# Sixteen attention units of a decode step: fourteen of them as one hardware loop of seven rounds, with the value and MLP products at other places

## The chip, the cores and the metric

The kernel runs on one core of one Trainium2 chip. Time is device time in microseconds (us) of one execution. In the profile, PE is TensorE (PEld its weight loads), DVE is VectorE, ACT is ScalarE, POOL is GpSimd and SP is SyncE, which here only issues transfers. PEclk is the clock granted to TensorE, 1.00 being full speed.

## What is computed

Two branches meet in the output. A is attention for one new token per batch (2 batches, 32 query heads, 8 KV heads, 32,768 cached positions, head size 128); B is a small MLP whose result gates A. All inputs are bf16.

```python
xn = layernorm(x)                                   # x: 2 x 1 x 512
q = xn @ wq                                         # 512 x 4096, 32 heads of 128
scores = einsum("bhqd,bhkd->bhqk", q, k) * 128**-0.5
p = softmax(scores);  o = einsum("bhqk,bhkd->bhqd", p, v)
s = o @ wo                                          # 4096 x 512
# branch B for a sequence of one token: its shifted parts are zero, so x1 = xn
h2 = gelu(layernorm(xn) @ w3) @ w4                  # F = 1792
out = x + s * silu(xn + h2)
```

K and V are 134 MB each; together with the weights the core reads 280.5 MB from HBM.

## The kernel before

**Units and buffers.** A unit is one batch and one KV head: 16 units, numbered 0 to 15, batch changing fastest. Each needs its K (8.39 MB) and its V (8.39 MB). `kbuf` has three chunks of half a K each. An even unit's K lies in chunks 0 and 1, an odd unit's in 1 and 2; even units work on chunk 1 first and then chunk 0, odd units on chunk 1 and then 2. So the next K can be loaded as soon as the first half of this K has been read. There is one V buffer, which first holds wq, w3 and w4. The last unit's V goes in three pieces into `kbuf` chunks 0 and 1, and wo in four pieces into chunk 2.

**The stream.** SP issues all large transfers in one order: half of K(0), wq, the other half, w3, w4, then K(1), V(0), K(2), V(1), ... K(15), V(14), V(15), wo. An instruction in that queue waits until its buffer has been read: a K for DVE's transposes (L320), a V for PE's value products (L348).

**A unit.** `k_job` takes a half of K in four pieces; DVE transposes a piece (L320) into one of two `ktb` buffers, and PE forms the scores from it in eight matmuls (`scores`, L268), one piece behind DVE. I call these eight matmuls a score block; a unit has eight blocks. After the last, DVE takes the maximum (L282), PE and DVE spread it over the partitions (mT L287, gm, gx, bc L298, nb L302), ACT does the exponential (L305) and DVE transposes the result (pT, L309). `v_job` then multiplies pT with V (64 matmuls of 16 rows in four column strips, L348), one unit behind: PE does the scores of unit n+1 and then the value products of unit n. `unit_end` copies the sum (acs, L365) and normalizes it (L369 to L376).

**The order** of all instructions is written out by hand in Python: the list `order` with `needs` for the transfers, and lists `waiting` and `glue` for score blocks and softmax steps that are put behind other work. Everything is unrolled: PE's program has 2,499 matmuls.

**The ends.** `q_job` (L404 to L418) makes the queries once wq is there; `mlp_job` (L437 to L469) runs both MLP products after unit 0's scores; V(0) may be loaded only after it. At the end `v_job` of unit 15, `o_final` (L382 to L388) and `wo_job` (128 matmuls, L395) follow, and two DVE instructions (L503, L505) and the output transfer.

Of the kernel before, what the change touches and what calls it, by code (L numbers as in the profile page):

```python
# [8 lines left out]
F32 = mybir.dt.float32  # L9
# [7 lines left out]
GT = 16  # L17
# [6 lines left out]
def kernel(  # L24
# [36 lines left out]
    units = [(b, g) for g in range(Hkv) for b in range(B)]  # L61
    NU = len(units)
# [8 lines left out]
    pt_pool = ctx.enter_context(tc.tile_pool(name="probT", bufs=2))  # L71
    tmp = ctx.enter_context(tc.tile_pool(name="tmp", bufs=3))
    sm_pool = ctx.enter_context(tc.tile_pool(name="small", bufs=3))
    sc_psp = ctx.enter_context(tc.tile_pool(name="sc_ps", bufs=2, space=bass.MemoryType.PSUM))
# [17 lines left out]
    def place(n, c):  # L92
        return (n % 2 + c) * CW

    def halves(n):
        return (0, 1) if n % 2 else (1, 0)

    loads = [("K", 0, 1), ("wq",), ("K", 0, 0), ("w3",), ("w4",)]
    for n in range(NU):
        if n + 1 < NU:  # L100
            loads += [("KK", n + 1), ("V", n)]
        else:
            loads += [("Z", n, c) for c in range(NCH)]
    wo_cuts = [0, NR // 2, NR - 6, NR - 2, NR]
    loads += [("wo",)]
    tiles = {}
    done = set()
    needs = {("V", 0): ("w4",), ("Z", NU - 1, 0): ("K", NU - 2, 0),
             ("Z", NU - 1, 1): ("K", NU - 1, 0), ("wo",): ("K", NU - 1, 1)}
    for n in range(1, NU):  # L110
        needs["V", n] = ("V", n - 1)
        needs["KK", n] = ("K", n - 1, halves(n - 1)[0])

    def issue_ready():
        while loads and needs.get(loads[0], None) in (done | {None}):
            issue(loads.pop(0))

    def issue(what):
        kind = what[0]
        if kind in ("wq", "V"):  # L120
            t = vslot.tile([128, NCH * CW], BF16, tag="v", name=f"slot_{kind}")
        elif kind in ("w3", "w4"):
            t = tiles[("wq",)]
        elif kind == "K":
            t = kbuf[:, place(0, what[2]):place(0, what[2]) + CW]
        elif kind == "KK":
            t = kbuf[:, place(what[1], 0):place(what[1], 0) + NCH * CW]
        else:
            c = 2 if kind == "wo" else what[2]
            t = kbuf[:, c * CW:(c + 1) * CW]  # L130
        if kind in ("K", "KK", "V", "Z"):
            b, g = units[what[1]]
            src = A_k_cache if kind[0] == "K" else A_v_cache
            sv = src[b, g, :, :].rearrange("(p t) d -> p (t d)", p=128)
            if kind in ("KK", "V"):
                nc.sync.dma_start(out=t[:, :], in_=sv)
            else:
                c0, w = what[2] * CW, CW
                if what == ("Z", NU - 1, NCH - 1):
                    w = w // 2  # L140
                for w0 in range(0, CW, w):
                    nc.sync.dma_start(out=t[:, w0:w0 + w], in_=sv[:, c0 + w0:c0 + w0 + w])
        elif kind == "wq":
            nc.sync.dma_start(
                out=t[:, 0:DK * HD].rearrange("p (k f) -> p k f", k=DK), in_=wq_v)
        elif kind == "wo":
            for r0, r1 in zip(wo_cuts, wo_cuts[1:]):
                nc.sync.dma_start(out=t[:, r0 * D:r1 * D], in_=wo_v[:, r0 * D:r1 * D])
        elif kind == "w3":
            nc.sync.dma_start(  # L150
                out=t[:, W3:W3 + DK * Fdim].rearrange("p (k f) -> p k f", k=DK), in_=w3_v)
        else:
            nc.sync.dma_start(
                out=t[:, W4:W4 + FK * D].rearrange("p (f d) -> p f d", f=FK), in_=w4_v)
        tiles[what] = t

    order = []
    for w in loads:
        order += [("K", w[1], c) for c in halves(w[1])] if w[0] == "KK" else [w]
    issue(loads.pop(0))  # L160
# [6 lines left out]
    issue_ready()  # L167
# [10 lines left out]
    qp = pers.tile([128, 4, B, Hkv, rep], BF16)  # L178
# [41 lines left out]
    layernorm(xn, xf, "ln1")  # L220
    xn_bf = tmp.tile([B, D], BF16, tag="row", name="xn_bf")
# [21 lines left out]
    g_sb = pers.tile([B, D], F32)  # L243
    g4 = pers.tile([128, 128], F32)
    nc.gpsimd.memset(g4[:, :], 0.0)


    unit_st = {}
    waiting = []
    glue = []  # L250

    def state(n):
        if n not in unit_st:
            unit_st[n] = {
                "sc": sc_psp.tile([128, NHALF, GT * 32], F32, tag="sc", name="sc"),
                "pT": None,
            }
        return unit_st[n]

    def scores(n, grp, ktb):  # L260
        b, g = units[n]
        st = state(n)
        half, sl = grp // NS, grp % NS
        sc = st["sc"]
        kv = ktb.bitcast(BF16).rearrange("p (t wb k two) -> p wb two t k", wb=2, k=32, two=2)
        off = 32 - rep - rep * sl
        for k in range(4):
            nc.tensor.matmul(  # L268
                sc[:, half, :].rearrange("p (t k) -> p t k", k=32),
                lhsT=qz[:, n % 2, k, off:off + 128],  # L270
                rhs=kv[:, k // 2, k % 2, :, :],
                start=(sl == 0 and k == 0), stop=(sl == NS - 1 and k == 3),
            )
        if sl == NS - 1 and half == halves(n)[1]:
            softmax_front(n)

    def softmax_front(n):
        st = state(n)
        if n + 2 < NU:
            place_q(n + 2)  # L280
        m1 = sm_pool.tile([128, 1], F32, tag="m1", name="m1")
        nc.vector.tensor_reduce(  # L282
            out=m1[:, :], in_=st["sc"][:, :, :].rearrange("p x k -> p (x k)"), axis=AX.X, op=ALU.max)
# [12 lines left out]
        def step2():  # L296
# [6 lines left out]
            S1 = sm_pool.tile([128, 1], F32, tag="S1", name="S1")  # L303
            pr = p_pool.tile([128, NHALF * GT * 32], BF16, tag="p", name="pr")
            nc.scalar.activation(  # L305
                out=pr[:, :], in_=st["sc"][:, :, :].rearrange("p x k -> p (x k)"), func=ACT.Exp,
                bias=nb[:, 0:1], scale=inv_sqrt_dh, accum_out=S1[:, :])
            pT = pt_pool.tile([128, NHALF * GT, 32], BF16, tag="pT", name="pT")
            nc.vector.transpose(out=pT[:, :, :].rearrange("p t r -> p (t r)"), in_=pr[:, :])  # L309
            st["pT"] = pT  # L310
            Sm = sm_pool.tile([128, rep], F32, tag="Sm", name="Sm")
            nc.vector.tensor_scalar_mul(out=Sm[:, :], in0=headm[:, :], scalar1=S1[:, 0:1])
            st["Sm"] = Sm
# [4 lines left out]
    def transposed(n, grp, kw):  # L318
        ktb = kt_pool.tile([128, KG * GT * DW], U32, tag="ktb", name="ktb")
        nc.vector.transpose(out=ktb[:, :], in_=kw)  # L320
        for x in range(KG):
            waiting.append((n, grp + x, ktb[:, x * GT * DW:(x + 1) * GT * DW]))
# [5 lines left out]
    def k_job(n, c):  # L328
        kw = kbuf[:, place(n, c):place(n, c) + CW].bitcast(U32)
        for blk in range(0, NB, KG):  # L330
            transposed(n, c * NB + blk, kw[:, blk * GT * DW:(blk + KG) * GT * DW])
            if n == 0 and c == 1 and blk < KTB * KG:
                if blk == (KTB - 1) * KG:
                    q_job()
                continue
            flush(LAG * KG)
            if glue:
                glue.pop(0)()

    def v_job(n, t, c0, c1):  # L340
        nx = NB // 4
        vv = t[:, :].rearrange("p (x i t d) -> p x t i d", i=4, t=GT, d=Dh)
        for x in range(c0 * nx, c1 * nx):
            half, r0 = x * 4 // NS, x * 4 % NS * rep
            pT = unit_st[n]["pT"]
            for u in range(GT):
# [3 lines left out]
                    lhsT=pT[:, half * GT + u, r0:r0 + 16],  # L350
# [4 lines left out]
        if c1 == NCH:  # L355
            unit_end(n)
# [4 lines left out]
    def unit_end(n):  # L361
        b, g = units[n]
        st = unit_st.pop(n)
# [3 lines left out]
        def step1():  # L367
            ot = mi_psp.tile([128, 2 * rep], F32, tag="mi", name="ot")
            nc.tensor.matmul(ot[:, rep:2 * rep], lhsT=ones_f[:, :], rhs=st["Sm"][:, :], start=True, stop=True)  # L369
            for i in range(4):  # L370
# [6 lines left out]
                out=oQ[:, b, g * rep:(g + 1) * rep], in0=ot[:, 0:rep], in1=rc[:, :], op=ALU.mult)  # L377
# [12 lines left out]
    def wo_job():  # L390
        w = tiles[("wo",)]
# [7 lines left out]
    def q_job():  # L399
        qT_ps = mi_psp.tile([128, Hq * B], F32, tag="mi", name="qT")  # L400
        for h in range(Hq):
            for k in range(DK):
                w = tiles[("wq",)]
                nc.tensor.matmul(  # L404
                    qT_ps[:, h * B:(h + 1) * B],
                    lhsT=w[:, k * HD + h * Dh:k * HD + (h + 1) * Dh],
# [5 lines left out]
        for k in range(4):  # L412
# [5 lines left out]
        nc.vector.tensor_copy(  # L418
            out=qp[:, :, :, :, :].rearrange("p k b g h -> p k (b g) h"),
            in_=qp_ps[:, :, :].rearrange("p (k u) h -> p k u h", k=4))  # L420
        place_q(0)
        place_q(1)

    def place_q(n):
        b, g = units[n]
        for i in range(4):
            c0 = 32 - rep + 32 * i
            nc.scalar.copy(  # L428
                out=qz[32 * i:32 * i + 32, n % 2, :, c0:c0 + rep], in_=qp[32 * i:32 * i + 32, :, b, g, :])

    def mlp_job():
        w3 = tiles[("w3",)][:, W3:W3 + DK * Fdim].rearrange("p (k q f) -> p k f q", k=DK, f=FK)
        w4 = tiles[("w4",)][:, W4:W4 + FK * D].rearrange("p (f d) -> p f d", f=FK)
        hT_ps = mi_psp.tile([128, FK * B], F32, tag="mi", name="hT")
        for f in range(FK):
            for k in range(DK):
# [5 lines left out]
                )  # L442
        hf = pers.tile([128, FK * B], F32)
        nc.vector.tensor_copy(out=hf[:, :], in_=hT_ps[:, :])
# [10 lines left out]
        h2_ps = mi_psp.tile([B, D], F32, tag="mi", name="h2")  # L455
        for f in range(FK):
            nc.tensor.matmul(  # L457
                h2_ps[0:B, :],
                lhsT=h_bf[:, f * B:(f + 1) * B],
                rhs=w4[:, f, :],  # L460
                start=(f == 0), stop=(f == FK - 1),
            )
        t_f = tmp.tile([B, D], F32, tag="row", name="t_f")
# [74 lines left out]
```

## Time and profile before

| | |
|---|---|
| median of 3 runs | 659.57 us (659.34 to 659.73) |
| the profiled execution's own time | 659.42 us |
| its span, first to last instruction | 657.6 us |
| PE busy | 375.9 us (57%) |
| DVE busy | 362.2 us (55%) |
| ACT busy, POOL busy | 38.5 us (6%), 2.4 us |
| read from HBM | 280.50 MB, 427 GB/s over the span |
| chain that ended last | DMA 67%, DVE 13%, PE 12% |

A column like "22.25 (x141)" in the windows view is busy time and number of instructions of an engine in that stretch; its last three columns are PEclk, the mean busy share of the 16 DMA engines (packets that overlap count twice, so it can pass 1) and GB/s. In the timeline a line has start, duration, engine, source line, operation, output<-input, count, and in brackets the idle time before it and what ended it. In the list of waits the three numbers are us in total, times and the longest.

### The profile page before, as it was taken

Reading aid. Unit: us, or ns where it says so; the run is one execution under the profiler, and the core shown is the slowest. Engines: PE = TensorE matmul, PEld = TensorE weight load, DVE = VectorE, ACT = ScalarE, POOL = GpSimd, SP = SyncE. Lnnn points to the kernel's source line nnn. Section 1 sums busy time; section 2 is a strip of 40 time slices with the busy share of each in tenths; the row PEclk is TensorE's granted clock in tenths of the full one; section 3 lists DMA queues with packets and bytes.
Section 4 is the critical chain, followed back from the end, with each engine's and each line's share of the span. In section 5 each row is a group of like instructions: output and inputs, shape, how many; then the busy total and the mean of one; then the engine's idle time right before and its main releaser. Section 6 shows DMA issues by size and latency. Waiting matters only on the chain.

```text
span 657.6 us, 5890 instructions
## 1 busy us (share of the span) xinstructions
PE 375.9 (57%) x2595; PEld 166.6 (25%) x2595; DVE 362.2 (55%) x312; ACT 38.5 (6%) x104; POOL 2.4 (0%) x10
## 2 busy tenths in 40 slices
PE   0583846638184673908558282754818376480865
PEld 0341322313132231303223031321303122130333
DVE  6183928547382754729356382936638284562821
ACT  1012010100001010000101000010100101000000
POOL 1000000000000000000000000000000000000000
PEclk9997987969587795968869596896959679695985
DMA  9999999999999999999999999999999999999995
GB/s 383 422 440 448 439 439 431 416 446 428 442 439 415 447 419 439 439 424 442 424 442 439 415 446 424 446 443 403 443 438 444 442 396 438 446 443 446 392 428 245
DMA packets 6125, 280.88 MB, mean 427 GB/s; under 512 B 714, under 2 KB 724, under 8 KB 980
## 3 DMA queue, kind: packets, MB, share of 16 engines
q1 hardware_dynamic: 6056, 280.50, 98.7%
q8 instruction: 20, 0.33, 0.2%
q14 instruction: 5, 0.04, 0.0%
q10 hardware_dynamic: 44, 0.01, 0.0%
HBM read 280.50 MB, written 0.00 MB: 427 GB/s over the span
## 4 chain that ended last, share of the span: by engine, by line
DMA 67%; DVE 13%; PE 12%; issue 6%; ACT 1%; ACTq 0%; SPq 0%; DVEq 0%
DMA kbuf<-in_A_k_cache_dram 60%; DVE ktb L320 12%; PE sc L268 10%; DMA kbuf<-in_A_wo_dram 4%; DMA slot_wq<-in_A_wq_dram 3%; PE h L457 1%; PE qT L404 1%; PE hT L437 1%; PE s_ps L395 0%; ACT L305 0%; DVE pT L309 0%; ACT pr L305 0%; ACTq L469 0%; ACT qz L428 0%; DVE g_sb L467 0%
## 5 line engine op out<-in xcount | busy, mean ns | idle before, releaser
L268 PE MATMUL sc<-ktb,qz 128*128 128x512 bf16 x1024 | 269.4, 412 | 228.1 <-DVE ktb L320 226.5
L320 DVE STREAM_TRANSPOSE ktb<-kbuf 128x2048 uint32<-128x2048 uint32 x128 | 285.0, 2282 | 156.1 <-DMA kbuf<-in_A_k_cache_dram 129.0
L268 PEld LDWEIGHTS <-qz 128*128 128x128 bf16 x1024 | 103.7, 102 | 387.4 <-issue 295.8
L348 PE MATMUL acc<-slot_V,pT 128*16 128x512 bf16 x960 | 54.4, 379 | 0.0
L428 ACT COPY qz<-qp 32x16 bf16<-32x16 bf16 x64 | 12.9, 201 | 444.4 <-PE sc L268 424.7
L282 DVE TENSOR_REDUCE m<-sc 128x1 f32<-128x1024 f32 x16 | 19.6, 1225 | 31.8 <-PE sc L268 31.8
L365 DVE COPY acs<-acc 128x512 f32<-128x512 f32 x16 | 11.1, 692 | 46.4 <-PE acc L348 46.4
L348 PEld LDWEIGHTS <-pT 128*16 128x16 bf16 x1024 | 24.5, 91 | 41.0 <-issue 14.5
L309 DVE STREAM_TRANSPOSE pT<-pr 128x1024 bf16<-128x1024 bf16 x16 | 19.9, 1245 | 22.6 <-ACT pr L305 22.6
L305 ACT ACTIVATE pr<-sc,nb 128x1024 bf16<-128x1024 f32 x16 | 17.8, 1113 | 134.3 <-DVE nb L302 134.3
L371 PE MATMUL ot<-sel,acs 128*128 128x4 f32 x128 | 17.4, 259 | 0.3 <-DVE acs L365 0.3
L371 PEld LDWEIGHTS ot<-sel,acs 128*128 128x128 f32 x128 | 16.4, 200 | 0.4 <-DVE acs L365 0.4
L298 PE MATMUL bc<-ones_f,gx 1*128 1x1 f32 x32 | 6.0, 256 | 17.9 <-DVE gx L292 17.9
L404 PE MATMUL qT<-xT,slot_wq 128*128 128x2 bf16 x128 | 3.6, 165 | 12.2 <-DMA slot_wq<-in_A_wq_dram 12.2
L348 PE MATMUL acc<-kbuf,pT 128*16 128x512 bf16 x64 | 6.4, 557 | 6.6 <-DMA kbuf<-in_A_v_cache_dram 5.0
L298 PEld LDWEIGHTS bc<-ones_f,gx 1*128 1x128 f32 x32 | 4.7, 182 | 20.9 <-DVE gx L292 20.9
L302 DVE TENSOR_SCALAR nb<-bc 128x1 f32<-128x1 f32 x16 | 2.5, 158 | 7.5 <-PE bc L298 7.5
L404 PEld LDWEIGHTS <-slot_wq 128*128 128x128 bf16 x128 | 3.5, 104 | 12.2 <-DMA slot_wq<-in_A_wq_dram 12.2
L369 PE MATMUL ot<-Sm,ones_f 128*128 128x4 f32 x32 | 6.4, 269 | 0.0
L457 PE MATMUL h<-slot_wq,h_bf 128*2 128x512 bf16 x14 | 4.8, 513 | 1.6 <-DVE h_bf L454 1.6
L369 PEld LDWEIGHTS ot<-Sm,ones_f 128*128 128x128 f32 x32 | 5.0, 195 | 1.1 <-issue 0.8
L410 DVE CAST q_sb<-qT 128x64 bf16<-128x64 f32 x1 | 0.2, 225 | 8.8 <-PE qT L404 8.8
(71 smaller groups left out, 65.2 us busy)
## 6 DMA issues: line engine op xcount, KB each, us to landing
kbuf<-in_A_k_cache_dram SPq DMA_DIRECT2D x2, 4096.0 KB, 31.7
slot_wq<-in_A_wq_dram SPq DMA_DIRECT2D x1, 4096.0 KB, 21.3
kbuf<-in_A_v_cache_dram SPq DMA_DIRECT2D x1, 4096.0 KB
kbuf<-in_A_v_cache_dram SPq DMA_DIRECT2D x2, 2048.0 KB
slot_wq<-in_B_w_dram SPq DMA_DIRECT2D x2, 1792.0 KB, 35.5
kbuf<-in_A_wo_dram SPq DMA_DIRECT2D x1, 2048.0 KB
kbuf<-in_A_wo_dram SPq DMA_DIRECT2D x1, 1280.0 KB, 27.3
kbuf<-in_A_wo_dram SPq DMA_DIRECT2D x1, 512.0 KB, 28.1
```

Of the source, the lines that this page charges most:

```text
L268: nc.tensor.matmul(sc[:, half, :].rearrange("p (t k) -> p t k", k=32), lhsT=qz[:, n % 2, k, off:off + 128], rhs=kv[:, k // 2, k % 2, :, :] ...
L282: nc.vector.tensor_reduce(out=m1[:, :], in_=st["sc"][:, :, :].rearrange("p x k -> p (x k)"), axis=AX.X, op=ALU.max)
L305: nc.scalar.activation(out=pr[:, :], in_=st["sc"][:, :, :].rearrange("p x k -> p (x k)"), func=ACT.Exp, bias=nb[:, 0:1], scale=inv_sqrt_dh ...
L309: nc.vector.transpose(out=pT[:, :, :].rearrange("p t r -> p (t r)"), in_=pr[:, :])
L320: nc.vector.transpose(out=ktb[:, :], in_=kw)
L348: nc.tensor.matmul(acc[32 * j:32 * j + 16, :].rearrange("p (i d) -> p i d", d=Dh), lhsT=pT[:, half * GT + u, r0:r0 + 16], rhs=vv[:, x - c0 ...
L365: nc.vector.tensor_copy(out=acs[:, :], in_=acc[:, :])
L369: nc.tensor.matmul(ot[:, rep:2 * rep], lhsT=ones_f[:, :], rhs=st["Sm"][:, :], start=True, stop=True)
L371: nc.tensor.matmul(ot[:, 0:rep], lhsT=acs[:, i * Dh:(i + 1) * Dh], rhs=sel[:, i, :], start=(i == 0), stop=(i == 3))
L404: nc.tensor.matmul(qT_ps[:, h * B:(h + 1) * B], lhsT=w[:, k * HD + h * Dh:k * HD + (h + 1) * Dh], rhs=xT[:, k, :], start=(k == 0), stop=(k ...
L428: nc.scalar.copy(out=qz[32 * i:32 * i + 32, n % 2, :, c0:c0 + rep], in_=qp[32 * i:32 * i + 32, :, b, g, :])
L457: nc.tensor.matmul(h2_ps[0:B, :], lhsT=h_bf[:, f * B:(f + 1) * B], rhs=w4[:, f, :], start=(f == 0), stop=(f == FK - 1),)
```

## The change

Units 1 to 14 become a hardware loop of seven rounds. A round holds two units: (batch 1, head m) and (batch 0, head m+1). Unit 0 stands before the loop, unit 15 behind it. Buffers that took turns by unit (scores, pT, sums) now have one fixed tile per batch. Addresses that depend on the head come from registers: the transfers' source, the column of `oQ`, and the query columns, which DVE first copies into a small tile `qn` before ACT spreads them into `qz` (in the unrolled kernel ACT read them directly).

Inside the loop a semaphore wait compares with a register that grows by the round's count of increments. Each of PE's 526 instructions in a round and each of DVE's 36 increments its engine's loop semaphore. In front of many waits stands a register operation (22 on PE, 31 on DVE per round). ACT loads its function table once per round. At the end of a round each engine raises its registers and branches back by itself; there is no barrier in the loop. Behind the loop SP waits for the final values of the loop's semaphores, four of its own transfers and those of DVE, ACT and PE; then all engines pass a barrier, in which POOL clears the loop's semaphores, and go on. V(14) is the last transfer that the loop issues.

Three pieces of work have other places. The value products of the unit before come after the sixth score block of a unit, not after the eighth. The first MLP product comes after the sixth block of unit 0, its GELU after the eighth transpose. The second MLP product is cut into four column strips of 128 columns (56 matmuls in place of 14), so that the gate comes out in the layout of the final product; xn is brought into that layout by two small transfers at the start, and the two transfers of the gate are gone.

```diff
-    for what in order:
-        if what[0] == "K":
-            k_job(what[1], what[2])
-        elif what[0] == "V":
-            flush(0)
-            while glue and unit_st[what[1]]["pT"] is None:
-                glue.pop(0)()
-            v_job(what[1], tiles[what], 0, NCH)
-            done.add(what)
-            issue_ready()
-            while glue:
-                glue.pop(0)()
...
+    def step(b, g, bn, gn):
+        u = unit(bn, gn, True)
+
+        def values():
+            v_job(b, vbuf[:, :], 0, NCH)
+            load_v(bn, gn)
+
+        k_half(u, halves(bn)[0])
+        load_k(b, g + 1)
+        k_half(u, halves(bn)[1], between=values)
+        flush(0)
+        unit_end(b, g)
+        run_glue()
+
+    first_unit()
+    with tc.For_i(0, NU // 2 - 1, 1, iteration_sync="reg_based") as m:
+        step(0, m, 1, m)
+        step(1, m, 0, m + 1)
+
+    G = Hkv - 1
+    u = unit(1, G, False)
+    k_half(u, halves(1)[0])
+    load_v_part(1, G, 0, 0, CW)
+    load_v_part(1, G, 1, 0, CW // 2)
+    load_v_part(1, G, 1, CW // 2, CW)
...
+    k_half(u, halves(1)[1], between=lambda: v_job(0, vbuf[:, :], 0, NCH))
+    load_wo()
+    flush(0)
+    unit_end(0, G)
+    run_glue()
+    for c in range(NCH):
+        v_job(1, kbuf[:, c * CW:(c + 1) * CW], c, c + 1)
+    unit_end(1, G)
+    run_glue()
+    o_final()
+    wo_job()
...
+    def k_half(u, c, between=None, first=None):
+        b = u[0]
+        kw = kbuf[:, place(b, c):place(b, c) + CW].bitcast(U32)
         for blk in range(0, NB, KG):
-            transposed(n, c * NB + blk, kw[:, blk * GT * DW:(blk + KG) * GT * DW])
-            if n == 0 and c == 1 and blk < KTB * KG:
+            transposed(u, c * NB + blk, kw[:, blk * GT * DW:(blk + KG) * GT * DW])
+            if first is not None and blk < KTB * KG:
                 if blk == (KTB - 1) * KG:
-                    q_job()
+                    first()
                 continue
             flush(LAG * KG)
-            if glue:
-                glue.pop(0)()
+            if between is not None and blk == NB // 2:
+                between()
...
+    def first_unit():
+        u = unit(0, 0, True)
+        k_half(u, halves(0)[0], first=q_job)
+        k_half(u, halves(0)[1], between=mlp_in)
+        load_k(1, 0)
+        mlp_gelu()
+        flush(0)
+        mlp_out()
+        load_v(0, 0)
+        run_glue()
+        mlp_gate()
...
+    def mlp_out():
+        w4 = vbuf[:, W4:W4 + FK * D].rearrange("p (f d) -> p f d", f=FK)
+        h2_ps = mi_psp.tile([128, 128], F32, tag="mi", name="h2")
+        nc.vector.memset(h2_ps[:, :], 0.0)
         for f in range(FK):
-            nc.tensor.matmul(
-                h2_ps[0:B, :],
-                lhsT=h_bf[:, f * B:(f + 1) * B],
-                rhs=w4[:, f, :],
-                start=(f == 0), stop=(f == FK - 1),
-            )
...
+            for j in range(4):
+                nc.tensor.matmul(
+                    h2_ps[32 * j:32 * j + B, :],
+                    lhsT=mlp["h"][:, f * B:(f + 1) * B],
+                    rhs=w4[:, f, 128 * j:128 * j + 128],
+                    start=(f == 0), stop=(f == FK - 1), tile_position=(0, 32 * j))
```

## The prediction, as it was put on record

> **What bounds the kernel now.** I read the page's slices first.
>
> ```profile
> PEclk9997987969587795968869596896959679695985
> DMA  9999999999999999999999999999999999999995
> ```
>
> The DMA engines are full in every slice but the last; no compute engine is. The windows view, cut at the times when DVE starts on a new K, shows one steady unit and the time after the last K has landed.
>
> ```profile
> core 0: us, PE busy (x) PEld busy (x) DVE busy (x) ACT busy (x) POOL busy (x), PEclk, DMA share, GB/s
> 526.60:565.20 38.60, 22.25 (x141) 9.53 (x141) 21.85 (x17) 2.01 (x6) 0.00 (x0) 0.81 1.01 435
> ...
> 605.00:624.40 19.40, 15.05 (x57) 5.83 (x58) 17.78 (x8) 0.00 (x0) 0.00 (x0) 0.84 0.99 430
> ```
>
> A unit (8.39 MB of K, 8.39 MB of V) takes 38.6 us at 435 GB/s, while PE works 22.3 us and DVE 21.9. So units are paced by the stream, and a change in a unit's work costs nothing while transfers stay queued ahead. The list of waits gives the margin:
>
> ```profile
> DVE ktb L320 <- DMA kbuf<-in_A_k_cache_dram: 129.0, 15, 10.5
> DVE acs L365 <- PE acc L348: 46.4, 16, 11.2
> ```
>
> DVE stands idle some 9 us before nearly every K. Last, the timeline from K(15) on (units are numbered 0 to 15), which the change rearranges:
>
> ```profile
> 609.53 0.33 SPq L142 DMA_DIRECT2D kbuf<-in_A_v_cache_dram  x1
> 611.07 13.28 DVE L320 STREAM_TRANSPOSE ktb<-kbuf 128x2048 uint32<-128x2048 uint32 x6 [1.56 <-PE sc L268]
> 620.01 1.90 PE L268 MATMUL sc<-ktb,qz 128*128 128x512 bf16 x8 [0.28 <-DVE ktb L320]
> 626.22 3.63 PE L348 MATMUL acc<-slot_V,pT 128*16 128x512 bf16 x64
> 629.78 0.27 PE L287 MATMUL mT<-identf,m 128*1 128x128 f32 x1
> 634.29 2.67 PE L348 MATMUL acc<-kbuf,pT 128*16 128x512 bf16 x32 [1.62 <-DVE pT L309]
> 639.00 1.89 PE L348 MATMUL acc<-kbuf,pT 128*16 128x512 bf16 x16 [2.05 <-DMA kbuf<-in_A_v_cache_dram]
> 643.84 1.89 PE L348 MATMUL acc<-kbuf,pT 128*16 128x512 bf16 x16 [2.95 <-DMA kbuf<-in_A_v_cache_dram]
> 649.66 1.88 PE L395 MATMUL s_ps<-kbuf,oP 128*2 128x128 bf16 x64 [0.32 <-DVE oP L388]
> 651.73 2.23 PE L395 MATMUL s_ps<-kbuf,oP 128*2 128x128 bf16 x64 [0.19 <-DMA kbuf<-in_A_wo_dram]
> ```
>
> K(15) lands at 605.0. Its transposes, scores and softmax run **beside** the transfers of V(14) and V(15), so that after the last bytes (wo, 651.7) only 5.9 us follow. This overlap is the reader's key to the change.
>
> **Part 1: the head.** The first MLP product (56 matmuls, 3.47 us) now precedes the last two score blocks; the second becomes 56 matmuls of 128 columns in four column strips instead of 14 of 512 (4.75 us). The nearest row is wo's, 64 of that form in 1.88 us, so 1.65. PE: score block 6 ends at 42.5, +3.5 first product, +3.5 blocks 7 and 8, +1.7 second product = 51.2, and V(0) is issued there instead of at 56.59. K(1) is still streaming then: bytes up to its end are 24.64 MB, reached at 58.4 by the windows' rates. The old issue, 1.8 us ahead, left no visible hole (492 and 524 GB/s around 58). Worth 0 to -0.5 us; I take 0. The w3 and w4 loads now wait for a semaphore of x and of the first K half (which lands at 12.8); up to 22.5 wq still streams, so 0. If that cover went, each us would be one.
>
> **Part 2: one unit in the loop.** New order: six score blocks, the value products of the unit before, two score blocks, softmax. With K landing at 0, blocks end at 16.9 (620.01+1.90-605.00), V lands at 19.3, products end at 23.0, blocks at 26.6, and maximum 1.2, mT to pT 4.5 and the last small DVE steps 0.4 end the unit at 32.7. The next K lands at 38.6. With all data present and a warm clock the chain is 15.3 (six blocks) + 3.6 + 3.5 + 6.1 = 28.5 us, so it can stretch by **10.1 us a unit, 20 a round**, before it paces the stream. Into this margin go, per round: the branch back, some 50 register operations on PE and DVE, ACT's table load (1.28 us, after its wait for the scores, still ahead of exp), the qn copies on DVE, and a semaphore increment on each of PE's 526 instructions. The trace has no loop, so nothing prices these; they are bounded by 0 and the 20 us: cost 0.
>
> What is queued behind the waits: SP's next load, nothing else. K(n+2) needs the first half of K(n+1) transposed (10.3 us after its landing, with V in flight to 19.3); V(n+1) needs the value products (now at 23.0, formerly 24.6) with K(n+2) in flight to 38.6. Both stay queued ahead, so 14 units cost 0. That SP waits on older loads of the same buffer adds nothing: those have long been consumed.
>
> [...]
>
> **Part 3: the exit.** After the branch, SP waits for all four of the loop's transfer semaphores at their final counts, among them **V(14)**, then joins a barrier of all engines; DVE, PE and ACT are held in it. They finish unit 14 at about 600 and stand until V(14) has landed. Queued behind SP: the three V(15) loads and wo. Queued behind DVE: K(15), in its buffer since 605. V(14) lands at 605.0 + 19.4 = 624.4 (8.39 MB at the 430 of the window); bounds 624.3 (435 GB/s) and 626.2, where its products began without waiting. The barrier: the rows at both ends of the kernel show engine waits of 0.4 and 0.7 us; from the output's issue at 655.4 to the span's end, with a landing and two barriers, are 2.2. Between 0.3 and 2.2 I take 1.0, nearer the single barrier. Release R = 625.4. Then, serially:
>
> - six score blocks: 16.9 (same cold start as at 605)
> - value products of 14, present: 3.6; blocks 7 and 8: 3.6; maximum: 1.2
> - mT to pT: 4.5 (629.78 to 634.29)
> - value products of 15: 64 matmuls. Warm 3.63, all at half clock 4 x 1.89 = 7.56; the rows show the clock falling to 0.5 about 1 us after 634.29 and, at 141.0 and 607.5, recovering after 2.6 to 4.2 us of work: 5.4
> - sum to oP: 3.9 (645.73 to 649.66; 3.1 warm); wo: 2 x 1.88 = 3.8 (half that warm)
> - to the span's end: 3.6 (653.96 to 657.6)
>
> Sum 46.5, end 671.9 against 657.6: **+14.3**. The transfers do not bind: SP restarts at R, the stream has a hole of 2 to 3 us, and 12.6 MB at 430 GB/s have landed by R + 32, while wo is needed at R + 39.
>
> **Sum.** 0 + 0 + 14.3 on the profiled run's 659.42 gives 673.7, say 673.5; the median shown is 659.57, 0.15 more. Low end: everything warm (-1.8, -0.8, -1.9), R 0.8 earlier: 668.4. High end: products at half clock (+2.2), landing +1.8, barrier +1.2, and 0.8 if the code behind the loop starts as slowly as the kernel itself, whose first transfer is issued at 0.73: 679.7.
>
> **Rivals.**
> 1. *The loop paces the stream.* If branch, register waits and increments exceed 20 us a round, each us more costs 7. Against: PE has 16 us without work per unit. For: no row prices them, and PE's clock is at 0.5 at the head of each unit. With 2 us over a unit: 28 more, 701. Chance 0.04.
> 2. *The exit doesn't wait as I read it*: if the final counts were met a round early, the barrier would open at 600, K(15) start on its landing, and the tail run as now: 659.4 (+0.5 for the loads' restart). That is the change not having the drain it appears to have. Against: V(14)'s counter is among those waited for, with the last round's count. Chance 0.03.
> 3. *Faster.* Code loading takes 0.2% of the DMA engines (queue q8), 1.3 us; a loop held in the engines' buffers would give most of it back to the stream, and the earlier V(0) up to 0.5. It decides only where the exit costs under 1.8 us, thus only if unit 15 still overlaps V(14): 658. Chance 0.03. [...]
> 4. *The forecast*: 0.90, of which 0.82 lies inside 668.4 to 680.
>
> A measurement here can tell about 0.2% (1.3 us). Slower by more: 0.04 + 0.90 = 0.94; within: 0.03; faster: 0.03.
>
> **What would show it.** Right: the first transposes after the loop start at 625 to 627, after an idle of some 25 us; K landings in the loop 38.6 us apart; one dip of DMA in the slices near 625; PE waiting 2 to 3 us for V in the midst of each unit; about 46 us from the release to the end. Wrong: K landings further apart than 39 (rival 1), DVE starting K(15) at 605 (rival 2), or a tail near 42 us (clock warm) or over 50.

## The result, and the profile after

The changed kernel takes 669.86 us (median of 4 runs, 668.97 to 672.21) where the kernel before takes 659.65 us on the same chip (659.34 to 659.81): a ratio of 1.0153, 95% interval 1.0134 to 1.0172. The profiled execution took 669.03 us, its span is 667.2 us (before 659.42 and 657.6). The loss is 10.2 us where 14.3 was forecast; the time lies in the lower part of the stated range, 668.4 to 680.

The page's slices, clock and DMA:

```profile
PEclk9986978868697886869787785978778597875698
DMA  9999999999999999999999999999999999999791
```

DMA is full in all slices but the third from the end (7 tenths) and the last (1); before it was full in all but the last. The windows view, cut as before (a unit from K(13) to K(14); then the 19.3 us after the landing that K(15) should have, 563.90 + 38.6 = 602.5):

```profile
core 0: us, PE busy (x) PEld busy (x) DVE busy (x) ACT busy (x) POOL busy (x), PEclk, DMA share, GB/s
525.34:563.90 38.56, 22.86 (x141) 9.78 (x140) 21.93 (x18) 3.29 (x7) 0.00 (x0) 0.81 1.00 435
602.50:621.80 19.30, 0.00 (x0) 0.00 (x0) 0.00 (x0) 0.00 (x0) 0.00 (x0) 0.50 0.88 380
```

(The view books a packet of a transfer in the stretch in which it starts. The packets of K and V, 64 KB each, take 2.42 us in the loop, so bytes land a little later than its rows tell.) A unit in the loop is as long as before, at the same 435 GB/s. In the second row no engine works; the matching stretch before held 15.05 us of PE and 17.78 of DVE. Two lines in the list of waits are new, and DVE's waits for K are shorter (10.5 us at most before):

```profile
DVE ktb L281 <- DMA kbuf<-in_A_k_cache_dram: 71.1, 15, 6.3
...
PE acc L313 <- DMA vbuf<-in_A_v_cache_dram: 32.8, 14, 2.7
...
ACT L270 <- PEq L532: 26.0, 1, 26.0
```

PE now waits some 2.3 us for V in the midst of each unit, since its products come after the sixth block. The last line is ACT held behind the loop (PEq is PE's sequencer). The timeline from the end of unit 14 on shows DVE held there too:

```profile
597.88 0.16 DVE L337 TENSOR_TENSOR oQ<-ot,rc 128x4 f32 x1
...
622.44 4.51 DVE L281 STREAM_TRANSPOSE ktb<-kbuf 128x2048 uint32<-128x2048 uint32 x2 [24.40 <-PEq L532]
622.44 10.83 SPq L116 DMA_DIRECT2D kbuf<-in_A_v_cache_dram  x3
...
637.36 1.90 PE L232 MATMUL sc<-ktb,qz 128*128 128x512 bf16 x8 [0.29 <-DVE ktb L281]
639.19 3.63 PE L313 MATMUL acc<-vbuf,pT 128*16 128x512 bf16 x64
642.75 3.65 PE L232 MATMUL sc<-ktb,qz 128*128 128x512 bf16 x16
646.45 1.23 DVE L248 TENSOR_REDUCE m<-sc 128x1 f32<-128x1024 f32 x1 [4.75 <-PE sc L232]
...
651.90 5.74 PE L313 MATMUL acc<-kbuf,pT 128*16 128x512 bf16 x64 [0.81 <-DVE pT L273]
...
660.76 1.96 PE L356 MATMUL s_ps<-kbuf,oP 128*2 128x128 bf16 x128 [0.32 <-DVE oP L349]
```

DVE ends unit 14 at 598.0 and starts on K(15) at 622.44: 24.4 us in which the loop waits for its last transfer, V(14). SP is released in the same instant and only then asks for V(15). From there on everything is serial: scores, both value products, wo, end.

### The profile page after: what moved, and what is told of

Its sections match the earlier page's. It is cut to its first block, busy times and chain, and to the rows that moved or that the text cites. A ratio compares the mean times of both kernels' runs of the same rounds, so it can differ in the third digit from the quotient of the medians.

```text
span 667.2 us, 6746 instructions
## 1 busy us (share of the span) xinstructions
PE 391.4 (59%) x2637; PEld 175.0 (26%) x2637; DVE 362.1 (54%) x331; ACT 48.0 (7%) x115; POOL 2.5 (0%) x11
## 5 line engine op out<-in xcount | busy, mean ns | idle before, releaser
L313 PE MATMUL acc<-vbuf,pT 128*16 128x512 bf16 x960 | 69.2, 453 | 32.8 <-DMA vbuf<-in_A_v_cache_dram 32.8
L313 PEld LDWEIGHTS <-pT 128*16 128x16 bf16 x1024 | 30.7, 104 | 77.3 <-issue 60.5
L390 ACT COPY qz<-qn 32x16 bf16<-32x16 bf16 x68 | 13.7, 201 | 266.2 <-PE sc L232 246.4
L332 PE MATMUL ot<-sel,acs 128*128 128x4 f32 x128 | 20.6, 284 | 0.5 <-DVE acs L326 0.5
L332 PEld LDWEIGHTS ot<-sel,acs 128*128 128x128 f32 x128 | 19.7, 235 | 0.6 <-DVE acs L326 0.6
L253 PE MATMUL mT<-identf,m 128*1 128x128 f32 x16 | 4.3, 270 | 19.8 <-DVE m L248 19.8
L364 PE MATMUL qT<-xT,vbuf 128*128 128x2 bf16 x128 | 3.6, 165 | 11.7 <-DMA vbuf<-in_A_wq_dram 11.7
L364 PEld LDWEIGHTS <-vbuf 128*128 128x128 bf16 x128 | 3.5, 104 | 11.8 <-DMA vbuf<-in_A_wq_dram 11.8
```

What stands on the lines that cost most here:

```text
L313: nc.tensor.matmul(acc[32 * j:32 * j + 16, :].rearrange("p (i d) -> p i d", d=Dh), lhsT=pT_t[b][:, half * GT + u, r0:r0 + 16], rhs=vv[:, x ...
L332: nc.tensor.matmul(ot[:, 0:rep], lhsT=acs[:, i * Dh:(i + 1) * Dh], rhs=sel[:, i, :], start=(i == 0), stop=(i == 3))
L364: nc.tensor.matmul(qT_ps[:, h * B:(h + 1) * B], lhsT=vbuf[:, k * HD + h * Dh:k * HD + (h + 1) * Dh], rhs=xT[:, k, :], start=(k == 0), stop ...
L390: nc.scalar.copy(out=qz[32 * i:32 * i + 32, b, :, c0:c0 + rep], in_=qn[32 * i:32 * i + 32, :, :])
```

## The experiments

Ratios are to the kernel before on the same chip: 660.51 us (659.31 to 662.78) beside e1 to e4, 660.46 us beside e5 to e7.

**e1: the loop written out.** All other parts of the change stay.

```diff
-    with tc.For_i(0, NU // 2 - 1, 1, iteration_sync="reg_based") as m:
+    for m in range(NU // 2 - 1):
```

> The changed kernel with the loop written out as Python, so that no engine branches and no exit waits; tiles, placements and order of work are those of the changed kernel. Theory (the loop's exit is the whole cost; placements, fixed tiles and rounds cost nothing): back to the time before, 658 to 660.5 us, and DVE starts K(15) when it lands, near 604. Rival A (the placements or the fixed tiles cost something): stays above 663. Rival B (the loop helped the stream by loading less code): K landings come some 2.5 us later by unit 15 than in the loop, near 605 as before, and the time is above 659.5.

Measured: 659.62 us (12 runs, 659.33 to 660.24), ratio 0.9984 (0.9971 to 0.9996). The timeline at K(15):

```profile
605.05 4.50 DVE L281 STREAM_TRANSPOSE ktb<-kbuf 128x2048 uint32<-128x2048 uint32 x2 [6.17 <-DMA kbuf<-in_A_k_cache_dram]
```

K(15) is taken when it lands. That is 605.05 and not the 604 I had named: both signs set for rival B, K(15) near 605 and a time above 659.5, came true beside the theory's range, and are taken up below. The moved products and the MLP in strips are worth at most 0.3%, and the whole loss comes with the loop.

**e2: the last V outside.** In the loop, the load of V for batch 0 moves from the end of a round to the head of the next, so that the loop ends with K(15) as its last transfer, and V(14) is asked for behind it.

```diff
             v_job(b, vbuf[:, :], 0, NCH)
-            load_v(bn, gn)
+            if b == 0:
+                load_v(bn, gn)
...
     with tc.For_i(0, NU // 2 - 1, 1, iteration_sync="reg_based") as m:
+        load_v(0, m)
...
+    load_v(0, G)
```

> The loop stays, but each V load that stood at the end of a round stands at the head of the next one, and the last, V(14), behind the loop: the exit then waits for K(15) and V(13), not for V(14). Theory: release when K(15) lands, near 603; a hole of 2 to 3 us in the stream before V(14); unit 15 overlaps V(14) again and the tail runs as before: 659 to 662.5 us. Rival (rounds, register waits or code fetch cost the time): stays near 669.

Measured: 662.04 us (661.87 to 662.78), ratio 1.0023 (1.0012 to 1.0035). The timeline at the exit, then windows of 1 us around it:

```profile
602.92 2.31 DVE L281 STREAM_TRANSPOSE ktb<-kbuf 128x2048 uint32<-128x2048 uint32 x1 [5.31 <-PEq L534]
602.99 0.34 SPq L113 DMA_DIRECT2D vbuf<-in_A_v_cache_dram  x1
```

```profile
599.00:600.00 1.00, 0.00 (x0) 0.00 (x0) 0.00 (x0) 0.00 (x0) 0.00 (x0) 0.50 0.76 328
600.00:601.00 1.00, 0.00 (x0) 0.00 (x0) 0.00 (x0) 0.00 (x0) 0.00 (x0) 0.50 0.01 0
...
604.00:605.00 1.00, 0.00 (x0) 0.00 (x0) 1.00 (x1) 0.15 (x1) 0.00 (x0) 0.50 2.06 721
```

With the same loop the wait is 5.3 us instead of 24.4, and 7.8 of the 10.2 us between e1 and the changed kernel are back. What stays is a hole in the stream: no packet starts between 599.6 and 603.96. The packets then in flight end between 600.28 and 602.0, as one DMA engine after another runs out; the release comes 0.9 us later and the next packets 1.0 us after that, so an engine stands for 3.4 us on average. This loop waits for all its transfers, so none is in flight at its exit.

**e3: the wait without a loop.** The kernel before, with one small DVE copy that reads the end of V(14) ahead of K(15)'s first transpose.

```diff
+    held = pers.tile([128, 2], BF16)
...
+        if what == ("K", NU - 1, halves(NU - 1)[0]):
+            nc.vector.tensor_copy(out=held[:, :], in_=tiles[("V", NU - 2)][:, NCH * CW - 2:NCH * CW])
```

> The unrolled kernel before with one addition: ahead of K(15)'s first transpose DVE copies two columns out of V(14)'s buffer, so that it starts K(15) only when V(14) has landed. No loop, no barrier, SP's loads not held. Theory (unit 15 put in series behind V(14) is the price): K(15) starts near 624.5 and some 45 us follow: 670 to 673 us. Rival (branch, barrier or cold code behind the loop cost it): below 664.

Measured: 673.14 us (672.81 to 673.73), ratio 1.0189 (1.0164 to 1.0214). The timeline:

```profile
624.38 0.17 DVE L476 COPY held<-slot_V 128x2 bf16<-128x2 bf16 x1 [29.16 <-DMA slot_V<-in_A_v_cache_dram]
```

No loop, no barrier, no register, and the loss is there, 3 us larger than with the loop and a little above my range of 670 to 673; the serial rest after 624.46 takes 46.6 us to the span's end at 671.1. SP's loads were held too, other than I had expected: the last two pieces of V(15) were asked for at 628.99 and not at 609.53, since they wait for K(15)'s transposes. But nothing in the rest waits for a transfer. So the price is that of unit 15 starting after V(14).

**e4: five spare maxima a unit.** The changed kernel with 6.25 us of spare DVE work at the end of each unit of the loop; its results are unused.

```diff
         run_glue()
+        for _ in range(5):
+            nc.vector.tensor_reduce(out=spare[:, :], in_=sc_t[bn][:, :, :].rearrange("p x k -> p (x k)"), axis=AX.X, op=ALU.max)
```

> The changed kernel with five spare maxima on DVE (1.23 us each, 6.1 us) at the end of each of the loop's 14 units. Theory (a unit may stretch by 10 us before it paces the stream): the changed kernel's time, 668.5 to 672.5. Rival (the margin is the 4 to 6 us that DVE is seen idle before a K, or register waits and branches have eaten it): 5 to 25 us more.

Measured: 669.91 us (668.0 to 670.5), ratio 1.0141 (1.0116 to 1.0165), the time of the changed kernel. The timeline of a unit:

```profile
519.63 6.25 DVE L473 TENSOR_REDUCE spare<-sc 128x1 f32<-128x1024 f32 x5
525.98 4.50 DVE L281 STREAM_TRANSPOSE ktb<-kbuf 128x2048 uint32<-128x2048 uint32 x2
```

DVE's wait for K is used up, K(13) is taken 0.6 us late and K(14) 2.6 us (566.49 for 563.90), and the end does not move: 87 us of added work cost nothing. A margin of at least 6.25 us a unit is there; the forecast's 10.1 was not tried.

**e5 and e6: no margin.** The same with twelve maxima (14.8 us a unit), in the loop and written out, so that units take longer than the stream and a round's own cost must show.

> The changed kernel, with twelve spare maxima of the score tile on DVE at the end of each of the fourteen units of the loop (12 x 1.23 = 14.8 us a unit; results unused, the computation is otherwise unchanged). The chain of one unit, some 29 to 30 us without waits for transfers, becomes 43 to 45 us and outlasts the 38.6 us in which K and V stream, so that DVE and PE set the pace and nothing hides the loop's own round: the branch back, the register operations, the loading of code. Both theories expect 710 to 735 us. Mine (a round costs next to nothing): within 2 us of its unrolled twin, e6, K landings and DVE's gap at the end of a round (between the last spare maximum of an odd-numbered position and the next transpose) under 0.5 us, the wait for the last V at the exit nearly gone because V(14) lands during the spare work. Rival (the branch or the code loading stalls an engine for 2 us or more a round, hidden so far by the stream): 14 us or more above e6, with a gap of that size on DVE or PE once in two units.

> The same as e5 with the loop written out (a Python loop, no branch, no barrier, constant waits), the same spare maxima. It gives the time of fourteen units of 43 to 45 us without a loop: 710 to 735 us. Mine: e5 minus this is between -1 and +2 us. Rival (a stall in each round): this one is 14 us or more faster than e5; and if the unrolled code's loading is what costs, it is slower than e5.

Measured: e5 747.74 us (746.97 to 749.67), e6 732.6 us (730.59 to 735.51). e6 lies inside the range I gave, e5 far above it, and they are 15 us apart: by the letter of the expectations the rival's number. I took it apart in the profiled executions (spans 745.4 and 732.5, 12.9 apart). The exit takes 7.6: V(14) was asked for at 670.2, its last packet ends at 700.8, and the release is at 701.69, after a wait of 7.57 us on DVE. So my "nearly gone" was wrong. Some 5.9 us lie in the thirteen intervals from the maximum of unit 1 to that of unit 14 (585.25 and 579.39 us): 0.45 a unit, in PE's first score blocks. Windows of 2 us from the start of one such block in e5 (rows one, three and four), and of 1 us in e6 (two and four):

```profile
381.19:383.19 2.00, 2.00 (x5) 0.69 (x6) 2.00 (x1) 0.00 (x0) 0.00 (x0) 0.50 1.13 492
...
385.19:387.19 2.00, 2.00 (x6) 0.65 (x5) 1.92 (x1) 0.00 (x0) 0.00 (x0) 0.51 0.00 0
387.19:389.19 2.00, 2.00 (x11) 0.90 (x10) 1.42 (x1) 0.00 (x0) 0.00 (x0) 1.00 0.00 0
```

```profile
382.18:383.18 1.00, 1.00 (x4) 0.29 (x2) 1.00 (x1) 0.00 (x0) 0.00 (x0) 0.50 2.27 983
...
384.18:385.18 1.00, 1.00 (x7) 0.43 (x5) 0.72 (x1) 0.00 (x0) 0.00 (x0) 1.00 0.03 8
```

PE starts at 381.19 and 381.18. In e5 its clock goes from 0.50 to 1.00 after 6.0 us, in e6 after 2.75. Over the units of e5 this wait goes 6.0, 4.75, 4.0, 3.75, 3.0, 2.75 us and then 6.0 again, and its maxima repeat after six units, 269.66 us; in e6 it stays 2.75 for the last nine. The traces' records of the clock show why: in e5 every change, up or down, comes a whole number of steps of 3.413 us after the one before, and of the 54 stretches between changes in the changed kernel's trace all but the last, which the trace's end cuts off, last a whole number of them (3.41 to 34.13 us). 269.66 is 79 such steps, and e6's unit of 44.38 is 13. So in these traces the clock rises only at times that lie whole steps of 3.413 us apart, and a unit can fall into step with them, as e6's last nine did. Where both waited about equally (4.0, 3.75 and 3.0 or 3.25 us: PE's starts from 202.15 to 336.68 and from 202.40 to 336.77) three units take 134.53 and 134.37 us: 0.05 us a unit more with the loop.

**e8 and e9: the same, in step.** A cost of each round or the clock's steps? The twelfth maximum now reads half of the tile, which makes a unit some 0.6 us shorter.

```diff
-        for _ in range(12):
+        for _ in range(11):
             nc.vector.tensor_reduce(out=spare[:, :], in_=sc_t[bn][:, :, :].rearrange("p x k -> p (x k)"), axis=AX.X, op=ALU.max)
+        nc.vector.tensor_reduce(out=spare[:, :], in_=sc_t[bn][:, 0:1, :].rearrange("p x k -> p (x k)"), axis=AX.X, op=ALU.max)
```

> As e5, but the twelfth spare maximum reads only half of the score tile, so a unit has some 0.6 us less of spare work. In e6 the rise of PE's clock (0.50 to 1.00) came 44.39 us after the one before, 13 steps of 3.41 us, and each unit waited the same 2.75 us at half clock for it; in e5 the same wait went 6.0, 4.75, 4.0, 3.75, 3.0, 2.75 us and then 6.0 again, one step lost in six units. Theory (a round costs under 0.2 us; e5 lost its 0.45 us a unit by the place of its units on the clock's steps): with a unit that is short enough both kernels fall into units of 13 steps, 44.4 us from maximum to maximum, and the eight last intervals of this kernel and of its twin e9 agree within 0.1 us each. Rival (a stall of some 0.9 us a round, in the branch or the code): this kernel's intervals stay 0.4 us a unit above e9's.

> The unrolled twin of e8. Units of 44.4 us, with a longer wait at half clock than e6's 2.75 us (some 4 us), because what is taken from DVE's work is given back by an earlier start on the same steps: the time is that of e6, 729 to 734 us, though 8 us of work are gone. Theory: e8 differs from it only by the wait at the exit (7 to 8 us) and by under 1.5 us in the fourteen units. Rival: by 12 us or more.

Measured: e8 743.35 us, e9 730.02 us (one run each). The maxima of four units, first with the loop, then without:

```profile
445.19 1.23 DVE L248 TENSOR_REDUCE m<-sc 128x1 f32<-128x1024 f32 x1 [4.70 <-PE sc L232]
489.57 1.23 DVE L248 TENSOR_REDUCE m<-sc 128x1 f32<-128x1024 f32 x1 [4.70 <-PE sc L232]
533.93 1.23 DVE L248 TENSOR_REDUCE m<-sc 128x1 f32<-128x1024 f32 x1 [4.69 <-PE sc L232]
578.30 1.23 DVE L248 TENSOR_REDUCE m<-sc 128x1 f32<-128x1024 f32 x1 [4.70 <-PE sc L232]
```

```profile
442.32 1.22 DVE L248 TENSOR_REDUCE m<-sc 128x1 f32<-128x1024 f32 x1 [4.69 <-PE sc L232]
486.70 1.23 DVE L248 TENSOR_REDUCE m<-sc 128x1 f32<-128x1024 f32 x1 [4.70 <-PE sc L232]
531.07 1.22 DVE L248 TENSOR_REDUCE m<-sc 128x1 f32<-128x1024 f32 x1 [4.69 <-PE sc L232]
575.44 1.23 DVE L248 TENSOR_REDUCE m<-sc 128x1 f32<-128x1024 f32 x1 [4.70 <-PE sc L232]
```

44.37 us a unit in both, to 0.02, for the eight last intervals, as the theory asked. By itself this does not refute a stall: units in step hide it in a shorter wait for the clock, and that wait was 3.06 us with the loop and 3.38 without. What settles it is the part of a unit from its maximum to the next unit's first transposes, in which DVE waits for no rise of the clock. With the loop, for the units of the first two maxima above (the second ends round five, so the branch lies before 510.14):

```profile
465.67 4.49 DVE L281 STREAM_TRANSPOSE ktb<-kbuf 128x2048 uint32<-128x2048 uint32 x2
...
509.40 0.69 DVE L475 TENSOR_REDUCE spare<-sc 128x1 f32<-128x512 f32 x1
510.14 4.50 DVE L281 STREAM_TRANSPOSE ktb<-kbuf 128x2048 uint32<-128x2048 uint32 x2
```

Without, after the first maximum:

```profile
462.74 4.50 DVE L281 STREAM_TRANSPOSE ktb<-kbuf 128x2048 uint32<-128x2048 uint32 x2
```

That is 20.48 and 20.57 us with the loop and 20.42 without: 0.2 us a round, not 0.9. Over the branch 0.05 us lie between the spare maximum and the transposes; inside a round they overlap by 0.08. The two kernels are still 13.3 us apart, more than the 9.5 I allowed and by the letter the rival's 12 or more: 2.9 up to the maximum of unit 14 (1.3 of it already at that of unit 0), 7.9 for the exit, 2.5 in the tail, where the clock rose after 5.5 us in one and 3.4 in the other.

**e7: the exit earlier.** Six rounds in the loop, units 13 and 14 written out behind it.

```diff
-    with tc.For_i(0, NU // 2 - 1, 1, iteration_sync="reg_based") as m:
+    with tc.For_i(0, NU // 2 - 2, 1, iteration_sync="reg_based") as m:
...
+    step(0, NU // 2 - 2, 1, NU // 2 - 2)
+    step(1, NU // 2 - 2, 0, NU // 2 - 1)
```

> The changed kernel with six rounds in the loop; units 13 and 14 are written out behind it. The exit is 77 us earlier and waits for V(12) in place of V(14), about 545 us. Theory A (the price is the time for which no transfer is in flight, wherever the exit stands): after the release DVE has to transpose the first half of K(13), 9 us, before K(14) can be asked for, so the stream has a hole of 11 to 12 us that nothing gives back; K(14) begins to land 11 to 12 us late and the end moves by as much: 668 to 672 us, as with seven rounds. Theory B (what costs is that the work of the last unit is serial and has nothing behind it, so that an exit in the middle is covered by later units): 660 to 664 us.

Measured: 673.02 us (672.47 to 673.68), ratio 1.0181 (1.0150 to 1.0213). Windows before and after the release at 545.00, and DVE at K(14):

```profile
542.00:545.00 3.00, 0.00 (x0) 0.04 (x1) 0.00 (x0) 0.00 (x0) 0.00 (x0) 0.50 0.00 0
545.00:557.00 12.00, 8.94 (x31) 3.47 (x32) 10.53 (x5) 0.00 (x0) 0.00 (x0) 0.74 0.23 76
557.00:578.60 21.60, 14.10 (x111) 6.92 (x109) 11.29 (x14) 3.29 (x7) 0.00 (x0) 0.84 0.92 395
```

```profile
578.61 2.31 DVE L281 STREAM_TRANSPOSE ktb<-kbuf 128x2048 uint32<-128x2048 uint32 x1 [3.80 <-DMA kbuf<-in_A_k_cache_dram]
```

Theory A, and a little more than it asked: the stream stands for some 14 us (13.7 for a DMA engine on average), since K(14) can be asked for only when half of K(13) has been transposed (555.5). I had left out that the DMA engines run out from 542.2 to 544.1, up to 2.8 us before the release, and that the first packet of K(14) starts 1.0 us after its issue. K(14) is taken 14.7 us later than in the changed kernel (563.90), and the end is 13.1 us behind e1's. Here an exit in the middle isn't covered by what follows: this stream, full up to the end, gave no time back.

## Why the prediction was right, step by step

**Bound (right).** Units are paced by the stream: 38.56 us at 435 GB/s, and 6.25 us of work more per unit did not move the end (e4).

**Head (no effect, as forecast; the reason partly off).** V(0) was to be issued at 51.2; it was at 53.41. The timeline:

```profile
52.19 0.17 DVE L426 MEMSET h<- 128x128 f32 x1
...
52.41 0.95 PE L429 MATMUL h<-vbuf,h_bf 128*2 128x128 bf16 x56 [1.51 <-DVE h L426]
```

I had counted PE's work and not that the strips' PSUM tile is cleared by DVE, behind the maximum: PE waited 1.5 us. Blocks 7 and 8 took 4.94 us, not 3.5, at a mean clock of 0.73, and the product itself 0.95, not 1.65. K(1) was taken at 61.58 (61.42 in e1), and K(2) 38.6 later: nothing hung on it.

**Loop (right, and now priced).** 0 was the value taken between 0 and 20 us a round. e8 and e9 put it near 0.2 us a round, e5 and e6 near 0.1. Where I took a warm clock, it often was not: in nine of the fourteen units the value products took 5.1 to 5.3 us, since the clock stood at 0.50 for part of them (from 584.5 to 587.9 in the second line), and e1 shows the same in eight. Both cases:

```profile
544.71 3.63 PE L313 MATMUL acc<-vbuf,pT 128*16 128x512 bf16 x64 [1.93 <-DMA vbuf<-in_A_v_cache_dram]
...
583.22 5.32 PE L313 MATMUL acc<-vbuf,pT 128*16 128x512 bf16 x64 [2.33 <-DMA vbuf<-in_A_v_cache_dram]
```

So the products of that unit end 24.6 us after K lands, not 23.0, and the unit 34.1, not 32.7; the stream hid it. The semaphores: at full clock the 64 value products take 3.63 us in the loop (at 544.71), where they and their 64 weight loads each have an increment, and 3.63 behind it (639.19) as well as in the kernel before (626.22): the increments add no time that the trace shows. Whether they ran beside the products the runs don't tell. Code loading, from the pages of the changed kernel and of e1:

```profile
q8 instruction: 7, 0.11, 0.1%
```

```profile
q8 instruction: 20, 0.33, 0.2%
```

Seven packets in place of 20, and none of the seven between 116 and 622 us, in which the last six rounds lie: no loading of the loop's code shows in them. So the gain that my third rival named may exist: K's in the loop come 38.6 us apart throughout, while the kernel before and e1 each have two intervals of 39.8 or 39.9 us (254.69 to 294.56 and 526.64 to 566.45 in e1). That is 2.5 us of stream. That the code's loading makes those two intervals is argued, not shown: each held one or two such packets, as the others did.

**Exit (right; three terms a little off).** R was forecast at 625.4 and came at 622.44, so my sign for it, first transposes at 625 to 627, failed by 2.6 us. The landing of V(14) was forecast at 624.4, which is where it is in the kernel without a loop (e3: 624.38); in the loop, whose stream lost no 39.8 us interval, it is 602.5 + 19.3 = 621.8, 2.6 less, and its last packet ends at 621.5. The barrier was put at 1.0; 622.44 - 621.8 leaves 0.6. The hole in the stream, put at 2 to 3 us, was 3.4 for a DMA engine on average, and nothing waited for it. The chain of 46.5 took 44.8: value products of 15 5.74 for 5.4, sum to oP 3.1 for 3.9 and wo 1.96 for 3.8, since PE's clock had risen again at 656.2, and the end after wo 4.5 for 3.6. In e3 the value products and wo took 6.40 and 3.35, and the chain 46.6, so how near 46.5 came was in part luck with the clock. The span's end was forecast at 671.9 and is 667.2: 2.6 for the landing, 0.4 for the barrier, 1.7 for the chain.

**Rivals.** The loop doesn't pace the stream (K's 38.6 us apart, and e4), the exit does wait (24.4 us on DVE), and unit 15 doesn't overlap V(14). Of the 9.7 us between the spans of e1 and the changed kernel, K(15) taken later gives +17.4 (605.05 to 622.44), a shorter rest after it, with nothing left to load that binds, -7.7.

**Open.** The changed kernel's runs spread over 3.2 us. Those of before spread over 0.5 beside them, but over 3.5 on the chip of e1 to e4 (e1's over 0.9). A serial tail whose products run at half or full clock by where they fall on the clock's steps could do that in the changed kernel; it wasn't tried. Nor was a loop whose exit leaves a transfer in flight: the loop waits for all it has issued. No version here beats the kernel before by more than e1's 0.2%, and the fastest runs of the two are equal (659.33 and 659.31).

## What to carry to other kernels

A hardware loop's price need not be in its rounds (here some 0.2 us a round): ask which of its transfers is the last to land, since all engines of this loop stand at its exit until then (DVE 24.4 us, ACT 26.0), with nothing in flight. Put the last round's load behind the loop (e2 recovered 7.8 of 10.2 us), and reckon some 3 us of empty stream even so (3.4 for a DMA engine on average in e2). In a kernel bound by its stream, later work did not cover such a hole at the other place tried either (e7).

## What the hardware showed that I had not expected

PE's clock, once fallen to 0.50, rose in the traces of the changed kernel, e5, e6, e8 and e9 only at times that lie whole steps of 3.413 us apart: in the changed kernel's it stays at one value for 3.41, 6.83, 10.24, 13.65, 20.48, 23.89 or 34.13 us, that is 1 to 10 steps. With PE idle for 17.65 to 19.30 us in each unit (e5, e6, e8, e9), the wait for the rise was between 2.7 and 6.0 us, by where the unit fell; the 44.37 us of e8 and e9 are 13 steps, and e5's six units (269.66) 79. Kernels paced by their engines locked to these steps here: e6, e8 and e9, at 44.37 to 44.38 us a unit. Then two kernels take the same time per unit though one does more, and taking work out (e9 against e6, half a maximum a unit, 44.37 us against 44.38) gains nothing, while e5, with some 0.05 us a unit more than e6, fell out of step and took 0.45 us a unit more.
